# One sign's tanh in a PSUM bank, short-use work on the other bank, and the later batches' 24-point transform spread over four groups

## The chip, the cores and the metric

The kernel runs as one program on one core of a Trainium2 chip. The metric is the device time of one execution in microseconds (us): the median of three runs before the change is 3141.66 us, with 3138.18 us the lowest and 3144.11 us the highest.

## The reference

Eight batches of 3072 tokens with 256 values each go through three layers. The first takes the real part of a two-dimensional Fourier transform. The second is a feed-forward layer with h - tanh(h) between its two products. The third sends each token to one of eight experts and scales the result by the expert's gate.

```python
X = np.fft.fft(np.fft.fft(x, axis=1), axis=2).real          # x: 8 x 3072 x 256
h = X.reshape(24576, 256) @ w_in                            # 256 x 2048
y = (h - np.tanh(h)) @ w_out                                # 2048 x 256
logits = y @ w_gate; e = argmax(logits); gate = softmax(logits)[e]
out[token] = gate * (relu(y[token] @ w1[e]) @ w2[e])        # 8 experts, 1024 hidden
```

Every float32 product is made from high and low parts: a value is rounded to `hi`, the rest `lo` = value - `hi` is kept, and three products are added.

## The kernel before

**Two phases.** Phase 1 makes y for all tokens and writes each token as a row to the place of its expert in DRAM. Phase 2 reads the rows expert by expert and runs the third layer; the change does not touch it.

**Groups and steps.** Phase 1 goes through 24 groups, three for each batch. A group holds 512 pairs of tokens (k and -k, the two "signs"), so 1024 tokens. A group has 18 steps, and below "step f of group g" is counted from 0. The code is written in the order in which each engine is to work: no scheduler changes it, and each engine takes its own instructions in that order.

**A step.** TensorE (PE) makes `u` and `v` from the group's transformed operands `pqh`, `pql` and the folded weights `Mh`, `Ml` (lines 404 to 409, six products of 512 columns). VectorE (DVE) takes `us` = `u` + a rank-one term (line 414), then the two signs `h` = `us` - `v` and `us` + `v` (lines 423, 424). ScalarE (ACT) takes the tanh of each sign twice, as float32 `t` (line 432) and rounded as `hi` (line 433). One step later `lo` = `t` - `hi` is formed: the first sign's on GpSimd (POOL), the second's on DVE, both line 440. Then PE adds the products of `hi` and `lo` with `w_out` to four accumulators (lines 452 and 456, twelve products). Steps 16 and 17 have no tanh: their `us` and `v` give the linear part `lin`. In step 0 of the next group DVE subtracts the accumulators from `lin` (`out1`, line 460).

**PSUM.** Eight banks: `u`, `v`, four accumulators, and two, `m0` and `m1`, that `bank()` hands out in turn for short-use work. That work is, in a group: the last stage of the Fourier transform for the group after it (`dft`, line 313, two halves, both in step 0, and in step 14 of group 2), which ACT and DVE take out as `pqh` (line 340) and `pql` (line 341); the gate's logits (step 2), their transposes (step 3), and the ranks of the tokens within their experts (`rank`, step 6).

**Gate and rows.** DVE works out the gate in steps 4 to 7; the last of it, `place`, ends with the whole-number row addresses `gpi` (line 545). In steps 8 to 15 POOL completes one column of rows in each step (line 576) and scatters it (line 568).

**A later batch's 24-point transform.** The first stage of the Fourier transform of batches 1 to 7 works in a buffer `ya` or `yb` in SBUF. Its steps are put in a queue `fq` by step number, from the table of `when()`, and issued at the end of a step. There are 24 operations on 128 x 768 elements, additions and subtractions through a scratch tile `tt` (line 242), which run on POOL, one in each step, for batches 2 to 7. What is left (line 256) is 46 smaller operations on DVE: four `scalar_tensor_tensor` of 768 columns, then four calls of `three()`, each of which begins with x1 - x2 into `vv` and x1 + x2. For batch nb from 2 on the POOL part runs from step 0 of group 3nb-4, and the DVE part in groups 3nb-3 and 3nb-2, except in steps 0, 1, 2, 7, 16 and 17. Batch 1's part runs in groups 0 to 2. So group 2 carries DVE work of batch 1 and POOL work of batch 2; groups 5, 8, 11, 14 and 17 carry most of a batch's POOL part; groups 3, 6, ... 18 the end of it and the begin of the DVE part; groups 4, 7, ... 19 the rest. Groups 20 to 23 carry none.

Of the kernel before, what the change touches and what calls it, by code (L numbers as in the profile page):

```python
# [20 lines left out]
P = 128  # L21
# [5 lines left out]
# a row in DRAM: the low halves of its values, their high halves, gate and token, filled up  # L27
ROW = 272
# The rows of an expert come in a first block of 256, then in blocks of 512 and 256. With rows beyond
# the first 256 in pieces of 256, there are 88 to 95 pieces, and at least 40 pairs of one expert.  # L30
# [8 lines left out]
# 24-point classes: (k1 mod 8, k1 mod 3) -> k1; the other classes are mirror images  # L39
# [3 lines left out]
# row of a batch's buffer that holds the real and the sine part of class kb  # L43
# [11 lines left out]
def when(nb):  # L55
    """the steps of phase 1 that carry batch nb's transform: 24 on Pool, the others on DVE"""
    if nb == 1:
        steps = [t for t in range(12, 32) if t != 18]
        return [steps[i * 19 // 24] for i in range(24)], [32, 33, 34, *range(37, 41), *range(42, 50)]
    s = NSTEP * (NCH * nb - 4)  # L60
    return ([s + i + 2 * (i > 14) for i in range(24)],
            [t for t in range(s + 26, s + 52) if t % NSTEP not in (0, 1, 2, 7, 16, 17)])


def parts(kb, ka):
    """slots of a batch's buffer that hold the real and the sine part of class (kb, ka)"""
    if kb in (0, 4):
        return (ROWR[kb], 2 if ka else 0), ((ROWJ[kb], 1) if ka else None)
    return (ROWR[kb], ka), (ROWJ[kb], ka)
# [10 lines left out]
def shape_constants():  # L80
# [17 lines left out]
    # direct and mirrored columns (rows) to even and odd half (columns), for two columns at a time  # L98
# [6 lines left out]
    c96 = np.zeros((2, 2, 24, 32, 2, 2))                     # column, mirror, n1, slot, half, column  # L105
# [37 lines left out]
def layout_inputs(x, w_in, w_out, w_gate, w1, w2):  # L143
    n1 = np.array([[(8 * a + 3 * b) % 24 for a in range(3)] for b in range(8)])
    x4 = x.reshape(B, 24, P, D)[:, n1]                       # batch, b, a, n2, d
    mir = np.zeros((B, 8, 3, P, P), np.float32)
    mir[..., 1:] = x4[..., :P:-1]
    xh = np.concatenate([x4[..., :P], mir], -1)              # batch, b, a, n2, col
    xh = xh.transpose(0, 3, 1, 2, 4)                         # batch, n2, b, a, col
    # batch 0: (column, mirror, n1), column, n2  # L150
# [5 lines left out]
    xz = x[:, :, P].reshape(2, 96, P).transpose(1, 0, 2)     # (4 batches, n1), half, n2  # L156
# [17 lines left out]
def phase1(tc, a, bk, zscr, zny, base, small, ngrp=NGRP):  # L174
# [13 lines left out]
    def bank(shape, name):  # L188
        """the next of the PSUM banks for short use"""
        pool, tag = free_banks.pop(0)  # L190
        free_banks.append((pool, tag))
        return pool.tile(shape, F32, tag=tag, name=name)

    # ---- what stays for the whole phase
# [4 lines left out]
    # high and low parts of w_out, each in two halves; other data have the second one's place at first  # L199
# [20 lines left out]
    def wout(i, f, n=1):  # L220
        """the high or the low part of n f tiles of w_out"""
# [9 lines left out]
    def fft_tasks(y, v, tmp, eng):  # L231
        """24-point transform over the (b, a) slots of y as a list of steps, each some sizes and closures: the slots become
        the classes' real and sine parts, the sine parts of the even half (columns of j and
        256 - j added) with the other sign. eng names the engine of a step, tmp its scratch."""
# [25 lines left out]
        def three(kr, kj, real):  # L260
# [7 lines left out]
            e = eng(9, kr)  # L268
            each((e.tensor_tensor, v, x(1), x(2), ALU.subtract), (e.tensor_tensor, x(1), x(1), x(2), ALU.add))
# [15 lines left out]
        d13 = (y[:, 5], y[:, 7])  # L285
        t5 = tmp(5)
# [3 lines left out]
        two(4, t[:, 0], t[:, 1], pm_ops[::-1], (d13, d13))  # L290
        # R1, R3 = d0 +- c p ; J1, J3 = c q +- d2
# [3 lines left out]
        three(5, 7, False)  # L295
        three(2, 3, True)
        three(0, 1, False)
        three(4, 6, False)
        return out

    def dft_block(ps, y, blk, o, half, m0, m1):
        """one block of 128 slots of the last stage: half 0 from the even, 1 from the odd part"""
# [15 lines left out]
    # ================= groups of 1024 tokens  # L318
# [11 lines left out]
    def dft(g, half):  # L330
        """last stage of the transform for a group; returns what takes it from PSUM"""
# [13 lines left out]
    def nyq(b):  # L345
        """the token of k = N/2, which has no sine part, of batch b"""
# [9 lines left out]
    def nyq_u(f0, f1):  # L356
        """all batches' tokens of k = N/2 up to the tanh, in parts"""
# [8 lines left out]
    def nyq_h():  # L366
# [3 lines left out]
        t = hp.tile([P, KF, B], F32, tag="t", name="nyt")  # L370
# [9 lines left out]
    def nyq_t():  # L380
        """their products with w_out, a token per partition"""
# [35 lines left out]
    def combine(g, f, us, v):  # L417
        """U and V into the two signs of the token pair"""
# [8 lines left out]
    def tanh(hs):  # L427
        out = []
        for s in range(2):
            t = hp.tile([P, 512], F32, tag="t", name=f"t{s}")  # L430
            hi = sp.tile([P, 512], F32R, tag="hi", name=f"hi{s}")
            S.activation(t, hs[s], AF.Tanh)  # L432
            S.activation(hi, hs[s], AF.Tanh)  # L433
# [34 lines left out]
    def logits():  # L468
        # four column groups of the array work side by side
# [22 lines left out]
    # p tokens in each of n columns  # L492
# [9 lines left out]
    def gate2(p=P, n=8, twin=False):  # L502
# [7 lines left out]
        if twin:                         # token 0 is its own partner: counted once  # L510
# [12 lines left out]
    def rank(p=P, n=8):  # L523
        """places within the experts before the column's token, and in the last column the sums"""
# [9 lines left out]
    def place(p=P, n=8, twin=False):  # L534
# [10 lines left out]
        V.tensor_copy(pi, pf)  # L545
# [785 lines left out]
```

## Time and profile before

| | |
|---|---|
| median of three runs | 3141.66 us (3138.18 to 3144.11) |
| span of the profiled execution | 3140.0 us; the page gives no other time for it |
| PE busy | 3038.6 us, 97% of the span |
| DVE, ACT, POOL busy | 2420.2, 1636.2, 1437.9 us |
| granted TensorE clock, mean | 0.989 |
| phase 1 | to about 1970 us (`out1` of the last group starts at 1967.90 us) |

PE's busy time is a sum of pipelined matmuls with modelled ends, so 97% does not say that PE could not be faster. What a stage could give is read from the length of a group with the transform's work beside it and without. Lines such as L440 are lines of the kernel's source.

### The profile page before, as it was taken

How to read it: one execution, taken by the hardware profiler on the slowest of the kernel's cores; microseconds unless marked ns; L12 is line 12 of the kernel's file. 1: busy time of each engine (PE TensorE's matmuls, PEld its weight loads, DVE VectorE, ACT ScalarE, POOL GpSimd, SP SyncE). 2: the span in 40 equal slices, each digit the busy share in tenths (PEclk: the TensorE clock that was granted, in tenths of full speed). 3: DMA queues.
4: the chain of work that ended last, by engine and by line, in shares of the span. 5: the costliest groups of instructions: out<-in, count | busy, mean ns of one | idle time of the engine just before them, and what ended most of it. 6: DMA issues, size and time to landing. Idle time of an engine off the chain costs nothing.

```text
span 3140.0 us, 44984 instructions
## 1 busy us (share of the span) xinstructions
PE 3038.6 (97%) x15660; PEld 2485.2 (79%) x15660; DVE 2420.2 (77%) x3998; ACT 1636.2 (52%) x3142; POOL 1437.9 (46%) x1299
## 2 busy tenths in 40 slices
PE   7998999999999999999999999799999999999998
PEld 7775787787787787777788887688888888888886
DVE  7789888888888888888887666676676766767664
ACT  5453455555555555455455555455555555555553
POOL 4566646746746746746744444622222222222222
PEclk9999999999999999999999999899999999999999
DMA  5220112112112112112111111665555556655551
GB/s 180 78 72 23 27 34 69 32 34 69 32 34 70 32 33 71 29 35 72 28 35 35 35 35 32 189 170 155 176 163 155 153 153 176 163 155 154 157 156 40
DMA packets 301615, 278.05 MB, mean 89 GB/s; under 512 B 246046, under 2 KB 261446, under 8 KB 285894
## 3 DMA queue, kind: packets, MB, share of 16 engines
q1 hardware_dynamic: 282422, 222.08, 26.5%
q0 software_dynamic: 18848, 52.99, 4.8%
q8 instruction: 125, 2.05, 0.3%
q14 instruction: 108, 0.88, 0.1%
q10 hardware_dynamic: 112, 0.05, 0.0%
HBM read 168.28 MB, written 55.39 MB: 71 GB/s over the span
## 4 chain that ended last, share of the span: by engine, by line
PE 70%; DVE 12%; issue 5%; ACT 5%; DMA 1%; POOL 0%; DVEq 0%; POOLq 0%; ACTq 0%; SPq 0%
PE acc L452 14%; PE dn L1244 12%; PE acc L456 7%; PE dn L1246 6%; PE up L1231 6%; PE up L1233 6%; PE up L1232 6%; DVE h L423 3%; PE dps L313 2%; ACT hi L433 2%; ACT t L432 2%; DVE us L414 2%; PE u L406 2%; PE u L404 2%; PE u L405 2%
## 5 line engine op out<-in xcount | busy, mean ns | idle before, releaser
L432 ACT ACTIVATE t<-h 128x512 f32<-128x512 f32 x768 | 479.4, 624 | 880.7 <-DVE h L423 880.7
L440 POOL TENSOR_TENSOR lo<-t,hi 128x512 fp32r<-128x512 f32 x384 | 514.0, 1338 | 708.6 <-ACT hi L433 475.1
L1255 POOL DMA_INDIRECT out_dram<-y,i x200 | 235.2, 1176 | 849.2 <-DVE y L1251 341.5
L1244 PE MATMUL dn<-w2s,hh 128*128 128x512 f32 x1600 | 573.0, 398 | 0.0
L414 DVE SCALAR_TENSOR_TENSOR us<-zb,A,u 128x512 f32<-128x512 f32 x432 | 321.3, 744 | 250.0 <-PE u L406 244.1
L433 ACT ACTIVATE hi<-h 128x512 fp32r<-128x512 f32 x768 | 472.8, 616 | 0.0
L1246 PE MATMUL dn<-w2s,hl 128*128 128x256 f32 x1600 | 449.4, 281 | 0.0
L440 DVE TENSOR_TENSOR lo<-t,hi 128x512 fp32r<-128x512 f32 x384 | 392.8, 1023 | 32.6 <-ACT hi L433 28.7
L1244 PEld LDWEIGHTS dn<-w2s,hh 128*128 128x128 f32 x1600 | 301.3, 188 | 69.7
L1231 PE MATMUL up<-xh,w1h 128*128 128x512 f32 (+1 forms) x960 | 344.5, 359 | 9.7 <-ACT xh L1219 9.0
L1232 PE MATMUL up<-xl,w1h 128*128 128x512 f32 (+1 forms) x960 | 341.6, 356 | 1.3 <-DVE xl L1220 1.1
L1233 PE MATMUL up<-xh,w1l 128*128 128x512 f32 (+1 forms) x960 | 342.5, 357 | 0.0
L1251 DVE SCALAR_TENSOR_TENSOR y<-dn,gi,y 128x256 f32<-128x256 f32 x200 | 96.7, 483 | 302.2 <-ACT y L1250 302.1
L1250 ACT ACTIVATE y<-dn,gi 128x256 f32<-128x256 f32 x200 | 95.2, 476 | 423.1 <-PE dn L1246 419.0
L1246 PEld LDWEIGHTS dn<-w2s,hl 128*128 128x128 f32 x1600 | 302.6, 189 | 4.9
L1236 DVE SCALAR_TENSOR_TENSOR hl<-up,hh 128x512 fp32r<-128x512 f32 (+1 forms) x480 | 272.3, 595 | 33.8 <-ACT hh L1235 33.8
L1235 ACT ACTIVATE hh<-up 128x512 fp32r<-128x512 f32 (+1 forms) x480 | 239.0, 521 | 94.6 <-PE up L1233 94.1
L452 PE MATMUL acc<-hi,W0b 128*128 128x512 f32 x768 | 261.8, 405 | 17.5 <-ACT hi L433 15.0
L452 PE MATMUL acc<-hi,W0a 128*128 128x512 f32 x768 | 256.3, 407 | 7.3 <-ACT hi L433 6.8
L423 DVE TENSOR_TENSOR h<-us,v 128x512 f32<-128x512 f32 x384 | 259.7, 676 | 2.6 <-PE v L409 0.2
L424 DVE TENSOR_TENSOR h<-us,v 128x512 f32<-128x512 f32 x384 | 259.6, 676 | 0.0
L452 PE MATMUL acc<-hi,W1b 128*128 128x512 f32 x768 | 238.8, 392 | 0.0
(273 smaller groups left out, 6336.5 us busy)
## 6 DMA issues: line engine op xcount, KB each, us to landing
w<-in_w SPq DMA_DIRECT2D x120, 1024.0 KB
yb<-in_x SPq DMA_DIRECT2D x16, 768.0 KB
ya<-in_x SPq DMA_DIRECT2D x12, 768.0 KB
zb<-zscr SPq DMA_DIRECT2D x24, 256.0 KB
raw<-in_win SPq DMA_DIRECT2D x8, 512.0 KB
raw<-in_wout SPq DMA_DIRECT2D x8, 512.0 KB
out_dram<-y,i POOLq DMA_INDIRECT x200, 4.0
row<-pl SPq DMA_TRANSPOSE x184
```

The costliest lines, as they stand in the source:

```text
L414: V.scalar_tensor_tensor(us, zb[g], A128[:, f:f + 1], u, ALU.mult, ALU.add)
L423: V.tensor_tensor(hs[0], us, v, ALU.subtract)
L432: S.activation(t, hs[s], AF.Tanh)
L433: S.activation(hi, hs[s], AF.Tanh)
L440: e.tensor_tensor(lo, t, hi.bitcast(F32), ALU.subtract)
L452: T.matmul(acc[i, s], wout(wi, f)[:, c], hl[s][0], start=f == 0 and wi == 0, stop=False)
L1231: T.matmul(ps, w1h[:, k, c], xh[:, k], start=k == 0, stop=False)
L1232: T.matmul(ps, w1h[:, k, c], xl[:, k], start=False, stop=False)
L1233: T.matmul(ps, w1l[:, k, c], xh[:, k], start=False, stop=k == 1)
L1236: V.scalar_tensor_tensor(hl[:, m], ps, 0.0, hh[:, m].bitcast(F32), ALU.max, ALU.subtract)
L1244: T.matmul(ps.rearrange("p a d -> p (a d)"), hh[:, m, c], w2s[:, m].rearrange("p a d -> p (a d)"), start=m == 0, stop=False)
L1246: T.matmul(ps[:, 1], hl[:, m, c], w2s[:, m, 0], start=False, stop=m == 7)
```

## The change

- `tanh()` makes `hi` before `t` for each sign, and from step 8 of group 0 on the second sign's float32 tanh goes to a tile `tp` in PSUM bank `m0`. DVE's `lo` reads it from there. POOL's `lo` is as before.
- `m0` is taken from `bank()`: short-use work has `m1` alone until the last turn after group 23. The second half of `dft` moves to the step after the first (steps 0 and 1, in group 2 steps 14 and 15). Logits, their transposes, gate, ranks, rows and scatters come two steps later (`late`): logits in step 4, `place` in step 9, scatters in steps 10 to 17.
- The last conversion of `place` moves from DVE to POOL.
- For batches 2 to 7 the first two operations of each `three()` go to POOL (8 for a batch), with two `vv` buffers in turn. The batch's load moves to step 1 of group 3nb-5. POOL's 24 operations go to steps 0 (two), 1 to 9 and 17, over groups 3nb-5 (from step 6) to 3nb-2; two groups of every three have work of the transform on DVE, from step 1 of group 3nb-3 to step 16 of group 3nb-2, with steps 0, 1, 2, 7 and 16 no longer left out. For batch 2 POOL begins at step 0 of group 2. Batch 1 keeps its engines and nearly its steps.

```diff
 def when(nb):
-    s = NSTEP * (NCH * nb - 4)
+    s = NSTEP * (NCH * nb - 5)
+    slots = [s + NSTEP * g + t for g in range(4) for t in (0, 0, 1, 2, 3, 4, 5, 6, 7, 8, 9, 17)]
...
-    def fft_tasks(y, v, tmp, eng):
+    def fft_tasks(y, vs, tmp, eng, first=4):
...
             e = eng(9, kr)
+            v = vs[(kr + 1) // 2 % 2]
             each((e.tensor_tensor, v, x(1), x(2), ALU.subtract), (e.tensor_tensor, x(1), x(1), x(2), ALU.add))
...
         three(5, 7, False)
+        three(4, 6, False)
         three(2, 3, True)
         three(0, 1, False)
-        three(4, 6, False)
...
-    def tanh(hs):
+    def tanh(hs, room):
         out = []
         for s in range(2):
-            t = hp.tile([P, 512], F32, tag="t", name=f"t{s}")
             hi = sp.tile([P, 512], F32R, tag="hi", name=f"hi{s}")
-            S.activation(t, hs[s], AF.Tanh)
+            t = pm.tile([P, 512], F32, tag="m0", name="tp") if s and room else \
+                hp.tile([P, 512], F32, tag=f"t{s}", name=f"t{s}", bufs=2 - s)
             S.activation(hi, hs[s], AF.Tanh)
+            S.activation(t, hs[s], AF.Tanh)
...
-        V.tensor_copy(pi, pf)
+        G.tensor_copy(pi, pf)
...
-                free_banks.append((pm, "m0"))
                 nyq(0)
...
+        late = 0 if last else 2
+        if last:
+            free_banks.append((pm, "m0"))
...
-                if f == 2:
+                if f == late + 2:
                     logits()
...
-                if not last and 6 <= f < 14:
-                    rowT(f - 6, last)
+                if not last and 8 <= f < 16:
+                    rowT(f - 8, last)
...
-                if nxt and f == ((9, 10) if g == 0 else (14, 14) if g == 2 else (0, 0))[half]:
+                if nxt and f == ((9, 10) if g == 0 else (14, 15) if g == 2 else (0, 1))[half]:
                     dft(g + 1, half)()
...
-                if not last and 8 <= f < 16:
-                    rowS(f - 8)
+                if not last and f >= 10:
+                    rowS(f - 10)
...
-                                    lambda i, k, nb=nb: V if i == 9 or nb == 1 and (i < 4 and k == 0 or i in (6, 7)) else G)
+                                    lambda i, k, nb=nb: V if nb == 1 and (i == 9 or i < 4 and k == 0 or i in (6, 7)) else G,
```

PE in steps 0 and 1 of group 7, before the change (`dps_0`, `dps_1` are the two halves of `dft`; L404 begins the next step):

```order
L313 MATMUL dps_0_6509<-gt,ya 128x128 x8
L313 MATMUL dps_1_6522<-gt,ya 128x128 x8
L404 MATMUL u<-pqh_0_5720,Mh 128x512
L405 MATMUL u<-pql_0_5721,Mh 128x512
L406 MATMUL u<-pqh_0_5720,Ml 128x512
L407 MATMUL v<-pqh_1_5733,Mh 128x512
L408 MATMUL v<-pql_1_5734,Mh 128x512
L409 MATMUL v<-pqh_1_5733,Ml 128x512
L452 MATMUL acc_6549<-hi_6498,W0a 128x512
L452 MATMUL acc_6550<-hi_6502,W0a 128x512
```

The same place in the changed kernel, up to step 1's products with `lo` and the second half:

```order
L334 MATMUL dps_0_6517<-gt,ya 128x128 x8
L425 MATMUL u<-pqh_0_5722,Mh 128x512
L426 MATMUL u<-pql_0_5723,Mh 128x512
...
L475 MATMUL acc_6551<-hi_6509,W1a 128x512
L479 MATMUL acc_6548<-lo,W0a 128x512
L479 MATMUL acc_6549<-lo,W0a 128x512
L479 MATMUL acc_6550<-lo,W0a 128x512
L479 MATMUL acc_6551<-lo,W0a 128x512
L334 MATMUL dps_1_6576<-gt,ya 128x128 x8
L425 MATMUL u<-pqh_0_5722,Mh 128x512
```

The second half now stands behind step 1's twelve products with `w_out` and no longer ahead of that step.

DVE in the same two steps before the change (`pql` is the low part of a `dft` half):

```order
L460 TENSOR_TENSOR lin_1268<-lin_1268,acc_5755 128x512
L341 TENSOR_TENSOR pql_0_6519<-dps_0_6509,pqh_0_6518 128x512
L341 TENSOR_TENSOR pql_1_6532<-dps_1_6522,pqh_1_6531 128x512
L414 SCALAR_TENSOR_TENSOR us<-zb_5693,A_98,u 128x512
L440 TENSOR_TENSOR lo<-t_6501,hi_6502 128x512
L423 TENSOR_TENSOR h_6565<-us,v 128x512
L424 TENSOR_TENSOR h_6566<-us,v 128x512
L414 SCALAR_TENSOR_TENSOR us<-zb_5693,A_98,u 128x512
```

And in the changed kernel:

```order
L483 TENSOR_TENSOR lin_1268<-lin_1268,acc_5744 128x512
L362 TENSOR_TENSOR pql_0_6527<-dps_0_6517,pqh_0_6526 128x512
L270 SCALAR_TENSOR_TENSOR yb<-vv,yb 128x128 x2
L435 SCALAR_TENSOR_TENSOR us<-zb_5695,A_98,u 128x512
L463 TENSOR_TENSOR lo<-tp,hi_6509 128x512
L444 TENSOR_TENSOR h_6564<-us,v 128x512
L445 TENSOR_TENSOR h_6565<-us,v 128x512
L362 TENSOR_TENSOR pql_1_6586<-dps_1_6576,pqh_1_6585 128x512
L270 SCALAR_TENSOR_TENSOR yb<-vv,yb 128x128 x2
L435 SCALAR_TENSOR_TENSOR us<-zb_5695,A_98,u 128x512
```

One `pql` went a step back, two pairs of the transform's operations came in, and `lo` reads `tp`.

POOL in steps 8 to 10 of group 8 before the change (`row` and `bk` are a column's completion and scatter):

```order
L440 TENSOR_TENSOR lo<-t_7675,hi_7676 128x512
L576 COPY row_7607<-ggi 128x16
L568 DMA bk<-row_7607,gpi 196608x272
L242 TENSOR_TENSOR tt<-ya 128x768
L440 TENSOR_TENSOR lo<-t_7726,hi_7727 128x512
L576 COPY row_7656<-ggi 128x16
L568 DMA bk<-row_7656,gpi 196608x272
L242 TENSOR_TENSOR tt<-ya 128x768
L440 TENSOR_TENSOR lo<-t_7771,hi_7772 128x512
```

And in steps 8 to 10 of the changed kernel's group 8:

```order
L463 TENSOR_TENSOR lo<-t_7652,hi_7651 128x512
L256 TENSOR_TENSOR ya<-tt 128x2x3x128
L463 TENSOR_TENSOR lo<-t_7712,hi_7711 128x512
L568 CAST gpi<-gpf 128x8
L256 TENSOR_TENSOR ya<-tt 128x2x3x128
L463 TENSOR_TENSOR lo<-t_7761,hi_7760 128x512
L599 COPY row_7692<-ggi 128x16
L591 DMA bk<-row_7692,gpi 196608x272
```

Scatters and the transform's operations no longer share these steps, and in step 9 a conversion of DVE's result stands ahead of a transform operation and of the next `lo`.

## Rows read from the trace of the kernel before

**Rows 1.** Stretches: groups 1, 2, 5, 6, 7, 21; from, to, length, busy (count), clock, DMA.
```profile
160.62:240.90 80.28, 77.25 (x366) 58.45 (x364) 72.67 (x106) 40.83 (x77) 52.93 (x41) 1.00 0.22 69
240.90:344.31 103.41, 85.94 (x389) 65.60 (x390) 95.71 (x135) 41.16 (x78) 65.67 (x48) 0.93 0.10 24
496.26:578.62 82.36, 79.11 (x379) 59.72 (x379) 66.18 (x93) 40.88 (x77) 64.17 (x48) 1.00 0.12 30
578.62:654.99 76.37, 75.25 (x378) 60.47 (x377) 63.94 (x107) 40.84 (x76) 46.96 (x39) 1.00 0.13 33
654.99:732.01 77.02, 76.03 (x378) 60.23 (x377) 69.61 (x125) 40.85 (x76) 35.84 (x33) 1.00 0.25 73
1749.37:1823.14 73.77, 73.77 (x377) 60.79 (x377) 51.61 (x92) 40.85 (x76) 32.42 (x32) 1.00 0.13 34
```

**Rows 2.** Waits in group 5: who waited for whom, us in total, times, longest.
```profile
PEld acc L452 <- ACT hi L433: 6.4, 11, 0.9
```

**Rows 3.** Groups of instructions in group 5: busy us, mean ns, idle before and releaser.
```profile
L440 DVE TENSOR_TENSOR lo<-t,hi 128x512 fp32r<-128x512 f32 x16 | 24.6, 1539 | 3.9 <-ACT hi L433 3.8
...
L424 DVE TENSOR_TENSOR h<-us,v 128x512 f32<-128x512 f32 x16 | 10.8, 675 | 0.0
```

**Rows 4.** Timeline of DVE and POOL in group 2: start, length, what.
```profile
313.82 3.63 DVE L256 TENSOR_TENSOR yb<-yb 128x256 f32<-128x256 f32 x1
...
314.07 1.85 POOL L242 TENSOR_TENSOR tt<-ya 128x768 f32<-128x768 f32 x1
...
315.87 1.29 POOL L440 TENSOR_TENSOR lo<-t,hi 128x512 fp32r<-128x512 f32 x1
```

**Rows 5.** Timeline of DVE in group 6, the transform's operation between two steps.
```profile
630.73 0.95 DVE L256 SCALAR_TENSOR_TENSOR yb<-tt,yb 128x768 f32<-128x768 f32 x1
633.01 0.69 DVE L440 TENSOR_TENSOR lo<-t,hi 128x512 fp32r<-128x512 f32 x1
...
637.10 0.83 DVE L440 TENSOR_TENSOR lo<-t,hi 128x512 fp32r<-128x512 f32 x1
```

**Rows 6.** Groups of instructions in group 2 (240.9 to 344.3 us).
```profile
L440 DVE TENSOR_TENSOR lo<-t,hi 128x512 fp32r<-128x512 f32 x16 | 21.7, 1355 | 0.4 <-ACT hi L433 0.4
```

**Rows 7.** Groups of instructions in group 1 (160 to 241 us).
```profile
L440 DVE TENSOR_TENSOR lo<-t,hi 128x512 fp32r<-128x512 f32 x16 | 17.3, 1083 | 1.4 <-ACT hi L433 1.2
```

**Rows 8.** Groups of instructions over the whole span.
```profile
L440 POOL TENSOR_TENSOR lo<-t,hi 128x512 fp32r<-128x512 f32 x384 | 514.0, 1338 | 708.6 <-ACT hi L433 475.1 <-issue 186.6 <-PE u L406 22.7
L432 ACT ACTIVATE t<-h 128x512 f32<-128x512 f32 x768 | 479.4, 624 | 880.7 <-DVE h L423 880.7
...
L242 POOL TENSOR_TENSOR tt<-yb 128x768 f32<-128x768 f32 x40 | 78.6, 1966 | 0.6
...
L340 ACT ACTIVATE pqh<-dps 128x512 fp32r<-128x512 f32 x48 | 27.2, 590 | 5.3 <-PE dps L313 5.3
...
L1254 POOL CAST i<-gi 128x4 int32<-128x4 f32 (+1 forms) x60 | 16.3, 272 | 0.0
```

**Rows 9.** Timeline of steps 0 and 1 of group 21.
```profile
1749.20 3.74 PE L313 MATMUL dps<-gt,yb 128*128 128x128 f32 x32
...
1752.69 0.48 PE L404 MATMUL u<-pqh,Mh 128*128 128x512 f32 x1
...
1753.16 1.28 DVE L341 TENSOR_TENSOR pql<-dps,pqh 128x512 fp32r<-128x512 f32 x2
...
1755.02 0.68 DVE L440 TENSOR_TENSOR lo<-t,hi 128x512 fp32r<-128x512 f32 x1
...
1755.96 1.07 PE L456 MATMUL acc<-lo,W0a 128*128 128x512 f32 x4
```

**Rows 10.** Timeline of steps 7 and 8 of group 21.
```profile
1783.03 0.22 DVE L542 TENSOR_REDUCE gpf<-gp 128x8 f32<-128x64 f32 x1
...
1783.80 0.83 DVE L545 CAST gpi<-gpf 128x8 int32<-128x8 f32 x1 [0.55 <-DVE gpf L542]
...
1786.35 1.07 PE L456 MATMUL acc<-lo,W0a 128*128 128x512 f32 x4
```

## What the change will do to the time

> **What bounds the kernel now.** I read the page's 40 slices first, then busy time by stretches, then for the stretches that differ the groups of instructions and the waits, and last the timeline of single steps. Phase 2 is untouched, so the question is what one group of phase 1 takes. Group 21, which carries nothing of the 24-point transform, takes 73.77 us with PE busy in all of it: this is PE's own pace, 73.77/18 = 4.10 us for a mean step, and it cannot be undercut by a change that takes no product away [rows 1]. Group 5 takes 82.36 us, group 6 76.37, group 7 77.02, and this triple comes back five times, group 18 and 19 ending the last one. So the transform's POOL part costs 8.6 us over the pace, its middle 2.6, its DVE part 3.25. Group 2 takes 103.41 us and group 1 80.28 [rows 1].
>
> Why is group 5 slow? DVE's `lo` has a mean of 1539 ns there; the addition of the same size that has one operand in PSUM takes 675 ns in the same group [rows 3], and `lo` itself takes 0.69 us when no transform operation is on POOL [rows 5]. The timeline of group 2 shows the mechanism: a DVE addition of 256 columns from SBUF to SBUF lasts 3.63 us and ends at 317.45 us, while two POOL operations run back to back to 317.16 [rows 4]. A DVE operation with two SBUF operands waits for POOL's operation, one with an operand in PSUM does not. A late `lo` makes the next `h` and so `hi` late, and PE waits for `hi`, 6.4 us in eleven waits in group 5 [rows 2].
>
> The Trainium skill says the same in "GPSIMD Engine Reference", section 1, Specifications: GpSimd's SBUF interfaces are shared with VectorE, with contention where a DVE instruction has two SBUF inputs. The traces agree: 1539 ns against 675 ns.
>
> **The change part by part.** The sum is made against the profiled execution, 3140.0 us of span and 1.7 us around it by the median: 3141.7 us. The median lies inside the three runs' spread of 6 us.
>
> *`tp` in PSUM, `hi` first.* DVE's `lo` falls to the 675 ns of its neighbour [rows 3]. ACT's writing to PSUM is not in the trace; its nearest rows are 624 ns from SBUF to SBUF and 590 ns for reading PSUM [rows 8]. I take 0.62 us; either end moves nothing, since ACT is busy 41 us of a group [rows 1]. With `hi` ahead of `t`, the second sign's `hi` ends one operation earlier, 0.5 us more room for the wait of rows 2. The new tile has one buffer, but the next tanh waits for `h`, which stands behind `lo` on DVE, so that wait is there already.
>
> *Eight operations for a batch from DVE to POOL, and DVE's rest spread over 33 steps.* In group 6 an operation of 0.95 us lies in every step and the steps still come at 4.09 us (633.01 to 637.10) [rows 5]. Over group 21's busy time DVE has 12.3 us more in group 6 and 18.0 in group 7 [rows 1]; over 33 steps that is under 1 us in a mean step, less than the 0.95 that is hidden there. So the DVE part is worth its 3.25 us, but not more.
>
> *The half of `dft` moved behind step 1's products.* This costs. In group 21 the first `lo` product starts at 1755.96, 6.76 us after `dft` [rows 9]. With half of 3.49 us (1749.20 to 1752.69) out of the way it would start at 1754.21, and its second, which needs DVE's `lo`, 0.23 us later, at 1754.44. DVE has one `pql` (0.64 us) less ahead of that `lo`, so it would run from 1754.38 to 1755.06 [rows 9]. PE waits 0.62 us, I take 0.65, in the 21 groups 1 and 3 to 22. What was hidden by the half is now waited for by PE itself.
>
> *The conversion on POOL.* It waits for DVE's `place` in step 9, and behind it on POOL stand a transform operation and the next step's `lo`, for which PE waits. In group 21 `place` ends at 1783.25 and the conversion of before starts at 1783.80. On POOL: 0.27 for it (the nearest conversion, rows 8), 1.97 for the transform, 1.34 for `lo`, so to 1787.38, while PE wants this `lo` at 1786.35 [rows 8, 10]. PE waits 1.0 us wherever POOL has a transform operation in step 9: group 2, the five of kind 5, five of kind 6 and five of kind 7. Without one it is 1784.07 + 1.34 = 1785.41, no wait.
>
> *Three transform operations on POOL in steps 17 and 0* take 3 x 1.97 us [rows 8], and then step 1's `lo` is due within 0.2 us of when PE wants it: 0.2 us.
>
> *Where two batches meet* (groups 4, 7, ... 19) a pair of DVE operations with two SBUF operands now stands in step 0 between `pql` and the `lo` for which PE waits. POOL is in the middle of that queue. If DVE gets in after the running `lo` it waits up to 1.34 us and works 0.5; if it loses as in rows 4, two operations of 1.34 us of `three()` go ahead as well, 4.5 in all. So 1.8 to 4.5 us; I take 2.5, below the middle of 3.15: rows 4 is a meeting that DVE lost, but in group 6 its operations between two steps were not held up at all [rows 5]. I add 0.3 for what follows in step 1, and 0.3 in the groups of kind 6 for the 0.95 us operation in their step 1.
>
> *Group 2.* `lo` falls from 1355 to 690 ns, 16 x 0.665 = 10.6 us [rows 5, 6], of a DVE that is busy for 95.7 of 103.4 us [rows 1], so on the path. POOL's operations leave steps 10 to 16, where a meeting like that of rows 4 (3.2 us over the 0.4 us of work) occurs twice: 6.4. The conversion's wait takes 1.0 back: -16. *Group 1*: 16 x (1083 - 690) ns = 6.3 us [rows 7], of which at most 5.9 lie over the pace with the new wait; I take 4. *Group 0*: one bank makes PE wait for two takings out at step 8, about 1.9 us, and `lo` gains as much: 0.
>
> The sum, group by group over the pace of 73.77:
> - groups 5, 8, 11, 14, 17: 73.77 + 0.65 + 1.0 + 0.2 = 75.6 for 82.4, five times -6.8: -34
> - groups 3, 6, ... 18: 75.7 for 76.4, six times -0.7: -4
> - groups 4, 7, ... 19: 73.77 + 0.65 + 1.0 + 2.5 + 0.3 = 78.2 for 77.0, six times +1.2: +7
> - group 2: -16; group 1: -4; groups 20 to 22: three times +0.65: +2
>
> Together -49 us: 3141.7 - 49 = 3093 us.
>
> **The rivals.**
>
> *The new waits don't bite.* Should `h` be earlier than in my working, every group comes to 74.2 us. For it speaks that group 21 shows not one wait on PE; against it that in group 21 the moved half still covers DVE. Gain 5 x 8.2 + 6 x 2.2 + 6 x 2.8 + 22 (group 2 to 81) + 6 (group 1) = 99: 3043 us.
>
> *One bank is too few.* PE would wait for ACT and DVE to empty `m1` (0.59 + 0.68 = 1.27 us by rows 8 and 9) at one use in each of 22 groups: +28 us, 3121. Against it: between the two halves of `dft` lie step 1's eighteen products, over 4 us, and the other uses are a step or more apart.
>
> The Trainium skill speaks for this rival: "Perfetto Trace Analysis", section Optimizing Tensor Performance, Matmuls, says that independent matmul groups should rotate through PSUM banks, so that emptying one overlaps the next group's matmuls. No run yet shows this work on one bank; by the rule the time is the 3121 us of the sentence above, by the distances in the order it is 3093.
>
> *Starvation, on the slow side.* POOL now has transform work in 12 slots of every group, also where DVE has its own; before, the two were mostly apart. Where both worked at once, in group 2, 29.6 us were lost, and taking DVE's `lo` out (10.6) leaves 19 us of meetings like that of rows 4 [rows 1, 4, 6]. If groups 4, 7, ... 19 become such groups, each pays 19 for my 2.8: 6 x 16.2 = 97 us more, 3190 us. It decides from 8.2 us for a batch on. Against it: in the mean step POOL's operation ends before DVE is through with `h`, and `three()`'s additions, the ones that met POOL, are on POOL now.
>
> *The change does nothing here*: if PE's waits in group 5 come from `hi` alone and `lo` is not what delays it: 3142. The timeline of group 2 speaks against it.
>
> **How the numbers follow.** My forecast, 3093 us with its own range of 3068 to 3115, has 0.50; the first rival 0.20; one bank, with all that lands between 3115 and 3135, 0.15; no effect 0.07; starvation 0.08. The range that leaves out no more than two in ten goes from 3043, the first rival's time, to 3130. A difference of 0.2% is 6.3 us, which is about what the spread of the runs lets one tell. Faster by more: 0.85; within: 0.07; slower: 0.08.
>
> **What would show it.** In the changed profile DVE's `lo` has a mean near 680 ns in every group; groups 5, 8, ... take 75 to 76 us, no longer the slowest kind; PE waits about 0.65 us for DVE's `lo` in step 1 of each group and about 1 us for POOL's `lo` in step 10; groups 20 to 22 are longer than before by the first of these alone. Waits of PE for `dps` to be emptied would show one bank as the price; DVE operations of `yb` or `ya` of 2 to 4 us in groups 4, 7, ... would show starvation. I am wrong if group 5's kind stays above 79 us.

## The result and the profile after

The changed kernel takes 3108.5 us (median of 4 runs, 3105.8 to 3112.5) against 3142.1 us: ratio 0.9895, interval 0.9881 to 0.9909. The forecast was 3093 us with a range of 3043 to 3130. The two profiled executions have spans of 3140.0 and 3110.7 us, 29.3 us apart; the one of the changed kernel is the slowest of its four runs.

Where the gain lies is read by stretches, as in [rows 1]: groups 1, 2, 3, 5, 6, 7 and 21 of the kernel after, with the same columns.

```profile
169.38:249.11 79.73, 75.05 (x366) 59.08 (x364) 64.18 (x106) 40.63 (x77) 50.47 (x43) 1.00 0.23 70
249.11:338.97 89.86, 79.76 (x389) 62.38 (x390) 81.27 (x135) 40.88 (x78) 55.58 (x45) 0.98 0.11 28
338.97:420.25 81.28, 76.12 (x382) 61.34 (x380) 61.53 (x107) 40.62 (x77) 49.75 (x44) 1.00 0.13 32
497.30:572.47 75.17, 74.49 (x380) 60.97 (x379) 50.43 (x92) 40.77 (x78) 51.03 (x45) 1.00 0.14 33
572.47:651.43 78.96, 75.94 (x382) 61.24 (x380) 62.16 (x112) 40.64 (x77) 46.56 (x43) 1.00 0.14 33
651.43:727.58 76.15, 75.10 (x370) 61.02 (x371) 56.15 (x111) 40.62 (x77) 47.08 (x44) 0.98 0.24 72
1723.09:1797.63 74.54, 73.98 (x378) 60.81 (x377) 50.36 (x91) 40.63 (x77) 29.93 (x33) 1.00 0.15 34
```

Group 5 falls from 82.4 to 75.2 us, group 2 from 103.4 to 89.9, group 7 from 77.0 to 76.2. Group 6 gets longer, 76.4 to 79.0, and group 3 too, to 81.3. Over all groups of each sort, measured so in both traces (kind 5 are groups 5, 8, ... 17, kind 6 groups 6, 9, ... 18, kind 7 groups 4, 7, ... 19):

| part | forecast, us | measured, us |
|---|---|---|
| kind 5, five groups | -34 | -35.7 |
| kind 6, six groups with group 3 | -4 | +17.4 |
| kind 7, six groups | +7 | -4.8 |
| group 2 | -16 | -13.5 |
| group 1 | -4 | -0.6 |
| groups 20 to 22 | +2 | +2.4 |
| start and group 0, group 23, phase 2 | 0 | +5.6 |
| sum | -49 | -29.2 |

Of the 20 us between the sums, kind 6 makes +21 and kind 7 -12; the rest is the start (+6) and groups 1 and 2, which gained 6 less than forecast, less 2 from kind 5.

DVE's groups of instructions in group 5 of the kernel after, which answer to [rows 3]:

```profile
L445 DVE TENSOR_TENSOR h<-us,v 128x512 f32<-128x512 f32 x17 | 11.5, 679 | 0.0
L463 DVE TENSOR_TENSOR lo<-tp,hi 128x512 fp32r<-128x512 f32 x16 | 10.9, 684 | 0.0
```

With an operand in PSUM `lo` takes 684 ns for 1539 and is no slower than `h`. Next, the waits of TensorE in the whole of group 6 of the kernel after (who, for whom, us in total, times, longest):

```profile
PE u L425 <- DVE us L435: 1.7, 1, 1.7
PE acc L479 <- DVE lo L463: 0.6, 1, 0.6
PE acc L479 <- POOL lo L463: 0.3, 1, 0.3
```

The second is the forecast's wait in step 1, the third the conversion's, the first was not forecast. The timeline of the kernel after shows the three: step 1 of group 6, the conversion's wait in group 6, then the end of the group (DVE, POOL and PE), and last a pair of DVE operations in step 0 of group 7.

```profile
576.85 0.97 PE L479 MATMUL acc<-lo,W0a 128*128 128x512 f32 x3 [0.58 <-DVE lo L463]
...
618.06 1.19 PE L479 MATMUL acc<-lo,W0b 128*128 128x512 f32 x4 [0.27 <-POOL lo L463]
...
643.04 0.41 DVE L270 SCALAR_TENSOR_TENSOR yb<-vv,yb 128x256 f32<-128x256 f32 x1
...
645.42 4.05 DVE L270 SCALAR_TENSOR_TENSOR yb<-vv,yb 128x256 f32<-128x256 f32 x1
649.39 0.73 DVE L435 SCALAR_TENSOR_TENSOR us<-zb,A,u 128x512 f32<-128x512 f32 x1
...
643.76 1.87 POOL L256 TENSOR_TENSOR yb<-yb 128x768 f32<-128x768 f32 x1
645.57 3.60 POOL L256 TENSOR_TENSOR yb<-tt 128x768 f32<-128x768 f32 x2
...
650.18 0.50 PE L425 MATMUL u<-pqh,Mh 128*128 128x512 f32 x1 [1.74 <-DVE us L435]
...
654.42 0.69 DVE L270 SCALAR_TENSOR_TENSOR yb<-vv,yb 128x128 f32<-128x128 f32 x2
```

At 643.04 a DVE operation of 256 columns with two SBUF operands takes 0.41 us. At 645.42 one of the same shape takes 4.05: POOL's three operations of steps 17, 0 and 0 run back to back from 643.76 to 649.17, and it ends 0.3 us after them. `us` stands behind it, TensorE behind `us`. The wait of 1.74 us is about half of the price (fix15, below, gives the whole: 3.7 us). Behind it the granted clock falls, by windows of the same trace: up to the wait's end, then behind it.

```profile
645.40:650.18 4.78, 3.04 (x23) 2.65 (x21) 4.72 (x3) 0.00 (x0) 3.77 (x3) 1.00 0.24 47
650.18:653.50 3.32, 2.89 (x8) 2.05 (x9) 3.27 (x6) 2.50 (x5) 1.26 (x2) 0.73 0.10 13
653.50:658.00 4.50, 4.25 (x19) 3.23 (x18) 4.06 (x8) 1.12 (x3) 2.69 (x3) 0.82 0.01 4
```

Granted clocks of 0.73 and 0.82, means between the two levels of 1.2 and 2.4 GHz, after a wait; full clock again in the following 7 us. Taken by the clock alone that is 3.32 x 0.27 + 4.50 x 0.18 = 1.7 us. This is not the other half of the price, though. At the same place behind group 9 the wait is 1.70 us and the clock stays at 1.00 (two waits of PE, then a window):

```profile
880.88 0.50 PE L425 MATMUL u<-pqh,Mh 128*128 128x512 f32 x1 [1.70 <-DVE us L435]
...
887.14 0.96 PE L479 MATMUL acc<-lo,W0a 128*128 128x512 f32 x3 [1.27 <-DVE lo L463]
```

```profile
880.88:884.20 3.32, 2.81 (x10) 1.74 (x11) 3.27 (x6) 2.49 (x5) 1.26 (x2) 1.00 0.00 0
```

Groups 9 and 10 are as long as groups 6 and 7 all the same (78.98 and 76.19 us). There TensorE waits 1.27 us for DVE's `lo` in step 1; behind group 6 that wait is 0.26. What is late in both is DVE, which is busy for 3.27 of the 3.32 us behind either wait. TensorE spends the time in idling or in slow products.

### The profile page after: what moved, and what is told of

It is laid out like the page before. It is cut to its first block, busy times and chain, and to the rows that moved or that the text cites. A ratio compares the mean times of both kernels' runs of the same rounds, so it can differ in the third digit from the quotient of the medians.

```text
span 3110.7 us, 44908 instructions
## 1 busy us (share of the span) xinstructions
PE 3007.3 (97%) x15660; PEld 2500.6 (80%) x15660; DVE 2224.6 (72%) x3925; ACT 1632.0 (52%) x3142; POOL 1412.2 (45%) x1372
## 5 line engine op out<-in xcount | busy, mean ns | idle before, releaser
L455 ACT ACTIVATE hi<-h 128x512 fp32r<-128x512 f32 x768 | 479.3, 624 | 835.9 <-DVE h L444 832.3
L463 POOL TENSOR_TENSOR lo<-t,hi 128x512 fp32r<-128x512 f32 x384 | 507.3, 1321 | 629.3 <-ACT t L456 500.1
L463 DVE TENSOR_TENSOR lo<-tp,hi 128x512 fp32r<-128x512 f32 x376 | 256.9, 683 | 3.7 <-ACT tp L456 3.7
L475 PE MATMUL acc<-hi,W0a 128*128 128x512 f32 x768 | 249.2, 405 | 0.4
L456 ACT ACTIVATE t<-h 128x512 f32<-128x512 f32 x392 | 241.4, 616 | 0.0
L479 PE MATMUL acc<-lo,W0a 128*128 128x512 f32 x768 | 215.8, 395 | 24.5 <-DVE lo L463 21.1
L475 PE MATMUL acc<-hi,W1a 128*128 128x512 f32 x768 | 238.9, 392 | 0.0
```

Of the source, the lines that this page charges most:

```text
L463: e.tensor_tensor(lo, t, hi.bitcast(F32), ALU.subtract)
L475: T.matmul(acc[i, s], wout(wi, f)[:, c], hl[s][0], start=f == 0 and wi == 0, stop=False)
L479: T.matmul(acc[i, s], wout(0, f)[:, c], hl[s][1], start=False, stop=f == KF - 1)
```

## The experiments

Two questions: which part of the change gives and which takes; and whether group 6 is long because DVE's operations meet POOL's or for another reason. All ratios are to the kernel before.

**bank_only: the first part alone** (`tp` on `m0`, one bank, `late`, moved half, conversion), with the transform's schedule of the kernel before.

```diff
-    s = NSTEP * (NCH * nb - 5)
-    slots = [s + NSTEP * g + t for g in range(4) for t in (0, 0, 1, 2, 3, 4, 5, 6, 7, 8, 9, 17)]
...
+    s = NSTEP * (NCH * nb - 4)
+    return ([s + i + 2 * (i > 14) for i in range(24)],
+            [t for t in range(s + 26, s + 52) if t % NSTEP not in (0, 1, 2, 7, 16, 17)])
```

> The change's first part alone: hi before t, the second sign's tanh in a PSUM bank, one bank for short-use work, gate and rows two steps later, the conversion on POOL; the 24-point transform keeps the engines and steps it had before the change. Theory: most of the gain is lo's PSUM operand, and the spreading takes out what is left: DVE's lo at about 680 ns everywhere, groups 5, 8, ... at 77 to 79 us (from 82.4), group 2 near 92, a wait of 0.6 us in step 1 of every group; 3118 to 3130. Rival: it is the spreading that gains, and the one bank with the moved half of dft costs 0.65 us in 21 groups: 3142 to 3156.

3098.7 us, 0.9868 (0.9852 to 0.9885): faster than the whole change. Groups 5, 6 and 7 by windows:

```profile
486.36:563.63 77.27, 76.19 (x380) 60.54 (x379) 50.40 (x92) 40.73 (x78) 61.17 (x51) 1.00 0.13 34
563.63:638.20 74.57, 74.00 (x378) 60.81 (x377) 57.74 (x107) 40.65 (x77) 44.67 (x40) 1.00 0.14 34
638.20:715.14 76.94, 75.31 (x378) 60.17 (x377) 68.44 (x124) 40.68 (x77) 31.15 (x33) 1.00 0.26 71
```

Group 6 is at the pace here. So its 79.0 comes from the spreading, which takes back 9.8 us in all: by the traces it costs kind 6 with group 3 28.7 us, and gives 11.5 in kind 5, 4.8 in kind 7 and 4 in group 2.

**spread_only: the second part alone**, on the kernel before: two banks, `t` in SBUF, one `vv`, so that a `three()` begins after the one before it (in the change two overlap).

```diff
-                              (r + 4, range(r + 5, half[0])), (r + 5, range(half[0], q + 1)),
-                              (q, range(q + 1, half[1])), (q + 1, range(half[1], end))]
+                              (r + 4, range(r + 5, half[0])), (half[0], range(half[0] + 1, q)),
+                              (q, range(q + 1, half[1])), (half[1], range(half[1] + 1, end))]
```

> The kernel before with only the second part of the change: the new transform schedule, with both PSUM banks, the second sign's tanh in SBUF and one vv. Theory: spreading puts GpSimd's transform operations beside every group's DVE lo, which has two SBUF operands here, so all three kinds become slow, as in tp_sbuf (78.7, 81.5, 84): 3175 us (3160 to 3190), slower than before. Rival (in tp_sbuf it was the single bank and the longer ACT path that cost, not the meeting of lo and GpSimd): the three kinds near 78.5 each, 3140 us (3125 to 3150).

3158.9 us, 1.0061 (1.0044 to 1.0077), a little below the theory's range and slower than before, as it said. The price is `lo`, in group 5:

```profile
L461 DVE TENSOR_TENSOR lo<-t,hi 128x512 fp32r<-128x512 f32 x16 | 18.9, 1179 | 1.3 <-ACT hi L454 1.3
```

All three kinds take 79 to 82.4 us (groups 3 and 19 less). Alone the first part is worth -43 us and the second +18; together they make -33.5, where the sum would be -25.

**tp_sbuf: the changed kernel with `tp` in SBUF**, and one `vv` to make room, with each `three()` behind the one before it as in spread_only.

```diff
-            t = pm.tile([P, 512], F32, tag="m0", name="tp") if s and room else \
-                hp.tile([P, 512], F32, tag=f"t{s}", name=f"t{s}", bufs=2 - s)
+            t = hp.tile([P, 512], F32, tag=f"t{s}", name=f"t{s}", bufs=2 - s)
...
+            vvs = [vv, vv]
```

> The change with the second sign's float32 tanh in SBUF again (one buffer), all else as in the change, but with a single vv, so that the four three() follow one another. Theory: DVE's lo goes back to 1000 to 1500 ns in groups with transform work on POOL, and groups 5, 8, ... take 78 to 80 us in place of 75.2; the time is 3125 to 3140. Rival: spread over four groups POOL's operations no longer meet lo, and PSUM gives nothing more: 3105 to 3113.

3187.9 us, 1.0143 (1.0126 to 1.0160), far above what was expected. `lo` in group 5 takes 1035 ns again, and the group 78.7 us for 75.2:

```profile
507.79:586.53 78.74, 75.22 (x380) 60.69 (x379) 57.73 (x93) 41.01 (x78) 55.50 (x45) 1.00 0.14 32
...
L462 DVE TENSOR_TENSOR lo<-t,hi 128x512 fp32r<-128x512 f32 x16 | 16.6, 1035 | 0.9 <-ACT t L455 0.8
```

Group 5 has none of the transform's operations on DVE, and POOL's 11 are the same in both kernels; so there the place of `tp` is the only difference, and 3.6 of the 7.2 us that the kind gained hang on it. The other groups also carry the single `vv` and its later `three()`, so the 79 us over the change are not the operand's price alone. The time is 29 us above spread_only; that kernel differs in the banks, the moved half and gate, the buffers of `t`, ACT's order and the conversion, and which of them makes the 29 us was not tried.

**step17: DVE's operation taken out of steps 17 and 0.**

```diff
-                              (r + 4, range(r + 5, half[0])), (r + 5, range(half[0], q + 1)),
+                              (r + 4, range(r + 5, half[0])),
+                              (r + 5, [t for t in range(half[0], q + 1) if t % NSTEP not in (17, 0)]),
```

> The change, with the one or two DVE operations of the transform that stood in step 17 of groups 3, 6, ... 18 (and in step 0 behind it) moved into the steps around them. Theory: in step 17 a DVE operation with two SBUF operands (0.42 us alone) lasts 4.05 us, because POOL runs three transform operations back to back from step 17 into step 0, and PE then waits for us; groups 6, 9, ... 18 go from 78.95 to about 75.9 us, and the time from 3108.5 to about 3090. Rival: the groups of this kind are long for another reason (the 0.95 us operation behind pql in step 1, the moved gate work), and the moved operation meets POOL elsewhere: 3104 to 3112.

3118.2 us, 0.9928 (0.9912 to 0.9945): slower than the change. The time that the theory gave was missed: kind 6 went to 81.8. Group 3 alone fell as it said, from 81.3 to 77.6. The timeline of its group 6 at the end (DVE, POOL, PE):

```profile
633.98 6.43 DVE L271 SCALAR_TENSOR_TENSOR yb<-vv,yb 128x256 f32<-128x256 f32 x2
640.33 0.73 DVE L436 SCALAR_TENSOR_TENSOR us<-zb,A,u 128x512 f32<-128x512 f32 x1
...
634.91 1.84 POOL L257 TENSOR_TENSOR yb<-yb 128x768 f32<-128x768 f32 x1
636.69 3.56 POOL L257 TENSOR_TENSOR yb<-tt 128x768 f32<-128x768 f32 x2
...
641.12 0.80 PE L426 MATMUL u<-pqh,Mh 128*128 128x512 f32 x1 [4.69 <-DVE us L436]
```

The operations of step 17 are now in step 16, and POOL's three run there: nothing in POOL's queue holds them back to their own step, so they start behind the group's last scatter, which POOL has issued while DVE is in step 16. Two small DVE operations (0.42 us the first) take 6.43, again to the end of the third. The mechanism is confirmed and the cure was too short by one step.

**cast_late: the conversion behind the transform operation of step 9.**

```diff
-        G.tensor_copy(pi, pf)
+        gs["pf"] = pf
...
+            if g > 0 and not last and f == late + 7:
+                G.tensor_copy(gs["pi"], gs["pf"])
```

> The change with the conversion of the row addresses on POOL issued behind the transform's operation of step 9 and no longer ahead of it. Theory: in step 9 POOL waits 3 us for DVE's place with a transform operation queued behind it, so that the next lo is late and PE waits 0.4 to 1.0 us in step 10 of 15 groups; without that wait the time falls by 6 to 12 us, to about 3099. Rival: PE's wait in step 10 is the transform operation's own length, and the time stays at 3106 to 3111.

3097.3 us, 0.9862 (0.9845 to 0.9878): 11 us better than the change, as the theory said. Groups 5, 6, 7 fall by 0.4, 0.6 and 0.9 us to 74.8, 78.4, 75.3, group 3 by 2.5.

**bank_cast: the same in bank_only.**

```diff
-        G.tensor_copy(pi, pf)
+        gs["pf"] = pf
...
+            if g > 0 and not last and f == late + 7:
+                G.tensor_copy(gs["pi"], gs["pf"])
```

> The first part of the change alone (bank_only, 3098.7 us, transform schedule as before), with GpSimd's conversion put behind the transform operation of step 9. Theory: the conversion's wait costs 0.4 to 1.0 us only where a GpSimd transform operation stands behind it, which in this schedule is group 2 and kind 5 alone: six times 0.6, 3095 us (3092 to 3097), kind 5 from 77.3 to 76.7, kinds 6 and 7 unchanged. Rival (the conversion's wait delays the next lo on GpSimd even without an operation behind it): all 20 groups gain 0.5, 3089 us.

3085.2 us, 0.9827 (0.9810 to 0.9843). The place was right, the price was not. Kinds 6 and 7 stay, but kind 5 gets 1.0 to 1.9 us a group shorter for the expected 0.6, and group 2 by 3.3. In this schedule POOL has an operation in each step from 10 to 14 too, and its queue does not catch up: in group 5 the `u` of steps 11, 12, 13 and 14 begins 0.4, 0.9, 1.3 and 1.8 us earlier than in bank_only.

**fix15: DVE's operations kept out of steps 15, 16, 17 and 0; fix15_cast: that and the conversion late.**

```diff
+    free = [t for t in range(r + 5, q + 1) if t % NSTEP not in (15, 16, 17, 0)]
...
-                              (r + 4, range(r + 5, half[0])), (r + 5, range(half[0], q + 1)),
+                              (r + 4, free[:len(free) // 2]), (r + 5, free[len(free) // 2:]),
```

> The changed kernel with two edits: GpSimd's conversion stands behind the transform operation of step 9 (as in cast_late, 3097.3 us), and DVE's transform work of a batch's two middle parts is kept out of steps 15, 16, 17 and 0 instead of step 17 alone being touched. Theory (a DVE operation with two SBUF operands is held exactly as long as GpSimd runs its three back-to-back operations of 128x768 from step 16's end on): no DVE operation is left there, so kind 6 falls from 78.4 to 75.5 us (five times -2.9) and group 3 by 3: 3097 - 17 = 3080 us (3076 to 3086). Rival (it meets GpSimd again wherever it is put, as in step17): kind 6 stays at 78 to 81, 3095 to 3112 us.

> The changed kernel with only DVE's transform work kept out of steps 15, 16, 17 and 0 of the two middle parts; the conversion as in the change. Theory (the two costs, held DVE operations and the conversion's wait, are separate and add up: conversion 11 us by cast_late, held operations 3097.3 - 3072.6 = 25 us by fix15_cast): 3108.5 - 25 = 3084 us (3081 to 3087), kinds 5, 6 and 7 at 75.2, 75.6 and 75.9. Rival (the conversion's wait costs only because DVE is late by the held operation): then fix15 alone brings most of both, 3076 us.

fix15 3087.0 us, 0.9824 (0.9808 to 0.9840): what the theory gave within 3 us. fix15_cast 3072.6 us, 0.9782 (0.9766 to 0.9798), below the theory's range and the best of all. The edits are worth 21.6 and 11.2 us alone, 35.9 together. With DVE's operations so placed the spreading gains: fix15 is 11.8 us below bank_only and fix15_cast 12.5 below bank_cast, which have the old schedule. Group 6 of fix15:

```profile
567.11:642.77 75.66, 74.69 (x378) 60.57 (x377) 59.94 (x112) 40.62 (x77) 45.62 (x43) 1.00 0.13 33
```

Step by step, the change's `u` is 1.9 us behind fix15's at the end of the wait of 1.74 us and 3.7 us behind from step 4 of group 7 on; of these 3.7, 3.3 show in the length of group 6. Behind group 9 it is 3.8, without the lower clock. Groups 3, 5, 6, 7 and 21 of fix15_cast by windows:

```profile
336.43:411.63 75.20, 74.25 (x378) 60.74 (x377) 59.02 (x107) 40.63 (x77) 48.46 (x44) 1.00 0.14 33
487.14:561.91 74.77, 74.20 (x380) 61.03 (x379) 50.46 (x92) 40.76 (x78) 51.04 (x45) 1.00 0.14 34
561.91:636.94 75.03, 74.33 (x378) 60.63 (x377) 59.87 (x112) 40.62 (x77) 45.48 (x43) 1.00 0.14 34
636.94:711.76 74.82, 74.25 (x377) 60.64 (x376) 55.77 (x110) 40.62 (x77) 48.08 (x45) 1.00 0.27 75
1685.00:1759.53 74.53, 73.94 (x378) 60.79 (x377) 50.38 (x91) 40.62 (x77) 29.91 (x33) 1.00 0.15 34
```

The groups shown are within 0.7 us of group 21, which has no transform. The timeline at the same place as before, the end of group 6 (POOL, then DVE):

```profile
632.61 1.87 POOL L257 TENSOR_TENSOR yb<-yb 128x768 f32<-128x768 f32 x1
634.42 3.63 POOL L257 TENSOR_TENSOR yb<-tt 128x768 f32<-128x768 f32 x2
...
632.84 0.69 DVE L445 TENSOR_TENSOR lin<-us,v 128x512 f32<-128x512 f32 x1
634.89 0.75 DVE L436 SCALAR_TENSOR_TENSOR us<-zb,A,u 128x512 f32<-128x512 f32 x1 [0.77 <-PE u L428]
```

POOL's three operations are unchanged. DVE's beside them (`lin`, `us`, `h`) all read PSUM and last 0.7 us, and DVE waits for TensorE, not the other way round.

**half_back: both halves of `dft` in step 0 again, still on one bank.**

```diff
-                if nxt and f == ((9, 10) if g == 0 else (14, 15) if g == 2 else (0, 1))[half]:
+                if nxt and f == ((9, 10) if g == 0 else (14, 15) if g == 2 else (0, 0))[half]:
```

> The changed kernel with both halves of the last transform stage in step 0 again, still on one bank. By the prediction: the wait of 0.6 us for DVE's lo in step 1 goes (21 times -0.6 = -13 us), and TensorE waits in its place for ACT and DVE to empty the single bank between the halves, 0.59 + 0.68 = 1.27 us in 21 groups = +27 us: 3108 + 14 = 3122 us (3115 to 3130), groups 20 to 22 at 75.3. Rival (TensorE's bank wait is longer, because DVE has lin and pql queued ahead: 2.5 us or more): 3145 us. Second rival (the emptying is hidden): 3096 us, groups 20 to 22 at 73.8.

3169.4 us, 1.0114 (1.0073 to 1.0156): the first rival's side, and beyond it. The timeline of group 22's beginning (PE, then DVE):

```profile
1847.02 1.95 PE L334 MATMUL dps<-gt,yb 128*128 128x128 f32 x16
1851.72 3.52 PE L334 MATMUL dps<-gt,yb 128*128 128x128 f32 x16 [2.75 <-DVE pql L362]
...
1848.59 2.47 DVE L483 TENSOR_TENSOR lin<-lin,acc 128x512 f32<-128x512 f32 x4
1850.98 0.68 DVE L362 TENSOR_TENSOR pql<-dps,pqh 128x512 fp32r<-128x512 f32 x1
```

The bank is emptied 2.75 us late, not 1.27: `pql` stands behind four additions of 2.47 us. After that wait the same 16 products take 3.52 us for 1.95; by windows, during the wait and for those products:

```profile
1849.00:1851.70 2.70, 0.00 (x0) 0.00 (x0) 2.66 (x5) 1.84 (x4) 1.27 (x1) 1.00 0.64 43
1851.70:1855.30 3.60, 3.58 (x17) 3.58 (x18) 0.00 (x0) 0.03 (x1) 0.00 (x0) 0.55 0.02 5
```

A granted clock of 0.55: almost all of the stretch at the lower level. So a group pays 3.8 us, 78.3 in group 21 for 74.5. In groups 11, 14 and 17 the same wait leaves the clock at 1.00, and they pay 2.2 us (77.3 to 77.4 for 75.2); group 11:

```profile
979.29 2.05 PE L334 MATMUL dps<-gt,ya 128*128 128x64 f32 x16 [2.76 <-DVE pql L362]
...
979.29:982.89 3.60, 3.60 (x24) 3.30 (x25) 0.88 (x2) 0.60 (x1) 1.08 (x1) 1.00 0.03 6
```

Group 5, of the same kind as 11, pays 3.7 with a clock of 0.59 over the 4 us behind its wait. So here the fall costs 1.6 us.

**t_first: `t` ahead of `hi` on ACT, as before.**

```diff
-            S.activation(hi, hs[s], AF.Tanh)
             S.activation(t, hs[s], AF.Tanh)
+            S.activation(hi, hs[s], AF.Tanh)
```

> The changed kernel with the tanh for lo (t, tp) ahead of the tanh for hi on ScalarE, as in the kernel before. Theory (the hi of a sign comes one operation of 0.6 us later, but the product with hi has slack in an undisturbed step, and lo needs both anyway): groups 20 to 22 stay at 74.5 to 74.8, only steps in which DVE is late lose 0.6 us: 3112 us (3108 to 3118). Rival (hi is what TensorE waits for in every step): 18 x 0.6 = 10 us a group, above 3200 us.

3117.2 us, 0.9927 (0.9910 to 0.9943): the theory's case. `hi` first is worth 8.7 us, a few tenths in a group of any kind (79.5 for 79.0, 76.7 for 76.2).

## Why the prediction was right, and where it was not

The time lies in the forecast's own range, and part of that is luck: kind 6 was 21 us dearer than forecast and kind 7 12 us cheaper.

*`tp` in PSUM.* Right in mechanism: 684 ns for 675 forecast, and tp_sbuf's group 5 is its proof from the other side. The size was right for the whole change, kind 5 -35.7 us for -34 and group 2 -13.5 for -16, but not all of it is the operand's: bank_only has -24.2 and -9.4 there, and the rest came with the spreading; 7.3 us of kind 5's 11.5 are the conversion's wait in the old schedule, by bank_cast. *`hi` first* was worth 8.7 us. Two rows were misread on the way. The 6.4 us of [rows 2] are waits of the weight loads, which overlap the products; the products' own waits for `hi` in group 5 of the kernel before are fewer:

```profile
PE acc L452 <- ACT hi L433: 2.3, 7, 0.5
```

And in group 6 an operation of 0.95 us lies in four steps, 8 to 11, not in every step.

*The moved half.* The wait of 0.58 us in group 6 and 0.6 in group 21 was forecast as 0.65, and groups 20 to 22 are 0.7 to 0.9 us longer. half_back shows what it buys net of this: 2.2 us in groups 11, 14 and 17, and 3.7 in groups 20 to 22, where the clock falls. The one-bank rival was right that emptying can cost, and it does not here, because of the distance between the halves: no wait of TensorE for the bank of `dps` shows in the trace. By the rule that the prediction took from the Trainium skill's "Perfetto Trace Analysis", section "Optimizing Tensor Performance", Matmuls, the time would have been 3121; the traces do not bear that out for this kernel, and do for half_back, with a wait of more than twice 1.27 us.

*The conversion.* Forecast at 1.0 us in 16 groups, measured by cast_late as 11 us in all, 0.4 to 0.9 a group and 2.5 in group 3: right in place, too dear by a third. In group 5 POOL's conversion starts 0.07 us behind `place`, for the 0.55 us that the forecast carried over from DVE's, and the conversion, the transform's operation and `lo` take 0.19 + 1.85 + 1.30 us for 0.27 + 1.97 + 1.34.

*Kind 7.* Forecast 78.2, measured 76.2. The step that was too dear is the pair in step 0, taken at 2.5: it got in between POOL's operations (654.42, 0.69 us for both) and cost under 1: in cast_late, with the pair in place, group 7 is 0.7 us longer than group 21.

*Kind 6, the step that failed.* "groups 3, 6, ... 18: 75.7 for 76.4": measured 78.9 to 79.0 and 81.3. I priced POOL's three operations in steps 17 and 0 by what they do to POOL's own next `lo`, 0.2 us in kind 5, and not by what they do to the DVE operation in step 17; the sum for kind 6, 73.77 + 0.65 + 1.0 + 0.3, has no term for them at all. I had looked at rival starvation, but in the groups of kind 7, and leaned on "in group 6 its operations between two steps were not held up at all [rows 5]". That row stands where POOL had no transform operation; it says nothing on a step in which POOL has three. fix15 takes group 6 from 78.96 to 75.66 and group 3 from 81.3 to 77.6 with no other edit than where DVE's operations stand, so the 3.3 us are shown to be this meeting. The Trainium skill's "SBUF — State Buffer", section "SBUF: two separate sides", has the pair of ports as an exclusive lock, held for a whole instruction by the one that starts first. The 4.05 us agree with being blocked. By the traces the DVE operation loses to a whole row of POOL operations; in step17 it does though the profile has it start 0.6 us before the first of them (while POOL was still issuing a scatter), so by these start times it is not the one that starts first.

*Starvation as a rival* was right in mechanism, wrong in place and in size (3.7 to 4.6 us in six groups, and not 16 in six).

*What stays open.* What decides whether the granted clock falls behind a wait was not found. The start up to the first group's end came 8.8 us later in this trace and phase 2 was 2.9 shorter; in six traces of kernels with this start (the change, step17, cast_late, fix15, fix15_cast, half_back) the first group ends between 164.6 and 169.4 us, and what sets it was not found. Group 1 gained 0.6 for 4; in bank_only it is 77.1, so the second part of the change takes the rest, but by which operation was not tried.

## What to carry to other kernels

An operand moved to PSUM keeps a DVE operation from being held up by GpSimd's (684 ns for 1539). The part of the change built on it gave -43 us alone; the spreading gave +18 without it, and with it paid only after DVE's operations were moved away from POOL's row of three. When work is spread, go through the steps in which the other engine has several operations in a row, and price what they hold up, not what they cost their own queue; an engine's operations begin when its queue lets them, which may be a step earlier than where they were written. Look at the granted clock behind a wait of TensorE, and compare with a like group where it did not fall before pricing it: it cost 1.6 us a group in half_back and nothing behind group 6, where DVE was late anyway.

## What the runs showed of the hardware

- The granted clock fell behind some waits of TensorE and stayed at 1.00 behind others of the same length: 0.73 and 0.82 behind one of 1.74 us (group 6 of the change) and 1.00 behind one of 1.70 (group 9); 0.55 behind one of 2.75 us (group 22 of half_back) and 1.00 behind one of 2.76 (group 11).
- A DVE operation of 256 columns with two SBUF operands took 0.41 us, and 4.05 beside three POOL operations in a row (the change, group 6); DVE operations with an operand in PSUM took 0.7 us beside the same three (fix15_cast, group 6).
- ACT wrote the tanh to PSUM in 580 ns and to SBUF in 616, by its groups of instructions in group 5 of the kernel after:

```profile
L456 ACT ACTIVATE t<-h 128x512 f32<-128x512 f32 x16 | 9.9, 616 | 0.0
L456 ACT ACTIVATE tp<-h 128x512 f32<-128x512 f32 x16 | 9.3, 580 | 0.0
```
